# Batch 0's second x load on ScalarE's DMA queue, between the state and the conv taps

## Chip, cores and metric

The kernel runs on one core of one Trainium2 chip. The metric is the device time of one execution in microseconds. TensorE (PE) multiplies, VectorE (DVE) and ScalarE (ACT) do the elementwise work, GpSimd (POOL) a little of it, SyncE (SP) issues most transfers; ScalarE can issue transfers too, on a queue of its own.

## The reference

Attention between tokens and a small state in both directions, then a feed-forward layer with a convolution and a gate:

```python
def _attn_ref(x, state):                     # x (8,8,512,64), state (8,8,32,64)
    scores = scale * np.matmul(x, state.transpose(0, 1, 3, 2))
    a = softmax(scores)                      # with 1e-09 in the sum
    xread = np.matmul(a, state)
    scores2 = scale * np.matmul(state, x.transpose(0, 1, 3, 2))
    a2 = softmax(scores2)
    sread = np.matmul(a2, x)
    return np.concatenate([xread, sread], axis=2)

def _moe_ref(x, w_in, conv_w, w_out):        # x (8,576,512)... through H*D = 512
    h = np.maximum(x @ w_in, 0.0)            # (.., 1024)
    conv_out = sum(conv_w[k] * shifted(h, k) for k in range(3))   # along the tokens
    gate = 1.0 / (1.0 + np.exp(-conv_out))
    return h * gate @ w_out
```

The outputs of the attention, 544 tokens for each of 8 batches, are the x of the second function. The weights `w_in`, `conv_w` and `w_out` arrive as 8-byte floats and are turned into 4-byte ones on the chip.

## The kernel before

The work is cut into some 1,650 operations (a load, a group of matmuls, one elementwise instruction or a few). Each is registered with its engine in `Plan`, and a table of numbers, `ORDER`, sets the one order in which all of them are written out; every engine then carries out its own share in that order, each waiting for what it needs. A `v` behind a number puts an operation that ScalarE could do on VectorE. A negative number stands for that many matmuls on zeros (tile `idle`).

The part that matters here is the first microseconds. Operation 0 loads the state of batch 0 (`st`, 64 KB) on ScalarE's queue, 1 the rest of the state. Operations 98 to 103 are the conv taps: 98 loads `conv_w` (24 KB, tile `raw`) on ScalarE's queue, 99 and 100 are ScalarE's two steps of the conversion (L243 `w_abs`, L246 `w_round`), 101 to 103 VectorE's three (L249, L252, L260), which leave the taps in `cw`. Operations 120 and 121 load the two halves of batch 0's x (`xt`, 512 KB each, four heads in each). 123 and 124 are the scores of batch 0 for the first and the second half of the tokens (L316 `first_scores`); each needs the state and both x loads. 125v and 126v copy these scores to SBUF on VectorE (L196, two instructions each). After them come transposes (L484), a row maximum (L488), the shift by it (L494), the maximum `nm` for the other softmax (L335), and the exponentials on ScalarE (L340, L504). 14, 2, 16 and on are w_in loads on SP's queue and their conversions. A w_in load that takes over the `raw` buffer of the taps waits until they are done.

The reduction that makes `heads` (L182) is set up ahead of the plan and is placed by the scheduler among VectorE's operations.

Of the kernel before, what the change touches and what calls it, by code (L numbers as in the profile page):

```python
# [55 lines left out]
PSUM = dict(ps=8)  # L56

ORDER = """
120 0 98 99 100 121 101 102 -5 103 -7 123 125v 124 126v -1 14 15 17 -1 16 140 141 148 2 3 4 -1 149 20 21 5 142 150 32
# [101 lines left out]
def fused_kernel(ctx: ExitStack, tc: tile.TileContext, xT, xn, stT, w_in, conv_w, w_out, out):  # L161
    nc = tc.nc
# [10 lines left out]
    def buf(shape, dtype, tag, name, **kw):  # L173
        return (work if tag in UNEVEN else even).tile(shape, dtype, tag=tag, name=name, bufs=SBUF.get(tag) or SBUF[tag[:-1]], **kw)
# [114 lines left out]
    at, ps_s, nm2, e2, ps_t, e2t, s2, ps_r, rr, ps_f, xts, xxs = ({} for _ in range(12))  # L289

    def xt_load(i):
        b, g = divmod(i, NG)
        xts[i] = buf([P, 2, S], F32, "xt", f"xt_{i}")
        nc.sync.dma_start(xts[i], xT[b, :, 2 * g:2 * g + 2, :])

    def x_load(b):
        xxs[b] = buf([P, NCH, DM], F32, "xx", f"xx_{b}")
# [82 lines left out]
    def attention(b):  # L380
        for g in range(NG):
            i = NG * b + g
            add("SP", "load_xt", partial(xt_load, i), w=[("xt", i)])
# [566 lines left out]
```

## Time and profile before

| | us |
|---|---|
| time, median of 3 runs (lowest to highest) | 355.45 (355.43 to 355.82) |
| time of the profiled execution | 355.52 |
| its span, first to last instruction | 353.7 |
| TensorE busy | 347.9 (98%) |
| VectorE busy | 317.8 (90%) |
| ScalarE busy | 259.2 (73%) |

The times are of whole executions, the views of one profiled execution; what they show is read against that one's span. Times in the views count from the first instruction. A row of a timeline gives start, length, engine, line, operation, the tile written and the tiles read, and in brackets how long the engine was idle before it and what ended that. In the profile q1 is SP's queue of transfers and q10 is ScalarE's.

### The profile page before, as it was taken

How to read it: one execution, taken by the hardware profiler on the slowest of the kernel's cores; microseconds unless marked ns; L12 is line 12 of the kernel's file. 1: busy time of each engine (PE TensorE's matmuls, PEld its weight loads, DVE VectorE, ACT ScalarE, POOL GpSimd, SP SyncE). 2: the span in 40 equal slices, each digit the busy share in tenths (PEclk: the TensorE clock that was granted, in tenths of full speed). 3: DMA queues.
4: the chain of work that ended last, by engine and by line, in shares of the span. 5: the costliest groups of instructions: out<-in, count | busy, mean ns of one | idle time of the engine just before them, and what ended most of it. 6: DMA issues, size and time to landing. Idle time of an engine off the chain costs nothing.

```text
span 353.7 us, 6691 instructions
## 1 busy us (share of the span) xinstructions
PE 347.9 (98%) x2538; PEld 274.1 (77%) x2538; DVE 317.8 (90%) x542; ACT 259.2 (73%) x557; POOL 30.3 (9%) x90
## 2 busy tenths in 40 slices
PE   8999999999999999999999999999999999999995
PEld 7776668687788877878878887788788788688884
DVE  1999999999998999999999999999867897899881
ACT  2999999999884798599386578837637583576573
POOL 1000000010000000010040011402001020101110
PEclk9999999999999999999999999999999999999999
DMA  7998979204000242032120100001100200020004
GB/s 257 395 374 330 340 243 373 77 1 150 11 20 2 92 158 109 3 119 92 53 97 2 59 32 1 0 3 60 59 24 30 79 19 30 2 90 1 0 32 148
DMA packets 12816, 35.06 MB, mean 99 GB/s; under 512 B 1520, under 2 KB 3696, under 8 KB 11760
## 3 DMA queue, kind: packets, MB, share of 16 engines
q1 hardware_dynamic: 12208, 34.28, 26.9%
q8 instruction: 20, 0.33, 0.4%
q10 hardware_dynamic: 576, 0.35, 0.3%
q14 instruction: 12, 0.10, 0.1%
HBM read 25.71 MB, written 8.91 MB: 98 GB/s over the span
## 4 chain that ended last, share of the span: by engine, by line
PE 90%; DVE 3%; ACT 3%; issue 0%; DVEq 0%
PE acc L701 47%; PE ps_h L626 22%; PE ps_hs L611 4%; PE ps_u L544 4%; PE acc_t L701 3%; PE ps_r L362 2%; PE ps_h L633 2%; PE ps_t L349 2%; PE acc_c L701 2%; PE acc L709 1%; PE ps_s L306 1%; ACT raw L246 1%; DVE nm L335 1%; ACT hc L243 1%; DVE hc L252 1%; DVE wi L260 0%
## 5 line engine op out<-in xcount | busy, mean ns | idle before, releaser
L701 PE MATMUL acc<-wo,g 128*128 128x512 f32 x726 | 173.4, 391 | 0.0
L701 PEld LDWEIGHTS acc<-wo,g 128*128 128x128 f32 x726 | 135.6, 188 | 30.3 <-issue 1.3
L626 PE MATMUL ps_h<-a,u 128*128 128x512 f32 x336 | 82.2, 390 | 0.0
L626 PEld LDWEIGHTS ps_h<-a,u 128*128 128x128 f32 x336 | 62.8, 188 | 13.8 <-ACT o L715 0.8
L678 ACT ACTIVATE t<-t 128x512 f32<-128x512 f32 x64 | 40.2, 631 | 20.9 <-DVE t L674 20.7
L205 ACT ACTIVATE g<-t 128x512 fp32r<-128x512 f32 (+1 forms) x62 | 38.2, 619 | 20.3 <-DVE t L683 20.1
L674 DVE SCALAR_TENSOR_TENSOR t<-h,cw,t 128x512 f32<-128x512 f32 (+1 forms) x64 | 47.3, 745 | 1.8
L669 DVE SCALAR_TENSOR_TENSOR t<-h,cw,t 128x511 f32<-128x511 f32 x64 | 47.4, 745 | 1.4 <-ACT t L194 0.9
L208 DVE TENSOR_TENSOR g<-t,g 128x512 fp32r<-128x512 f32 (+1 forms) x62 | 41.4, 672 | 7.5 <-ACT g L205 7.1
L200 ACT ACTIVATE h<-ps_h 128x512 f32<-128x512 f32 x61 | 36.0, 597 | 12.6 <-PE ps_h L626 11.5
L683 DVE SCALAR_TENSOR_TENSOR t<-t,h 128x512 f32<-128x512 f32 (+1 forms) x64 | 42.3, 667 | 3.1 <-ACT t L678 2.8
L194 ACT ACTIVATE t<-h,cw 128x512 f32<-128x512 f32 x47 | 33.9, 723 | 0.7
L644 POOL COPY hs<-h 128x1 f32<-128x1 f32 x40 | 12.7, 326 | 198.8 <-ACT h L200 180.2
L715 ACT ACTIVATE o<-acc 128x512 f32<-128x512 f32 (+1 forms) x31 | 16.7, 548 | 10.4 <-PE acc L701 9.7
L644 POOL COPY h<-hs 128x1 f32<-128x1 f32 x40 | 17.0, 437 | 35.9 <-DVE t L683 13.5
L208 DVE TENSOR_TENSOR u<-ps_u,u 128x512 fp32r<-128x512 f32 x28 | 18.8, 680 | 0.4 <-ACT u L205 0.4
L205 ACT ACTIVATE u<-ps_u 128x512 fp32r<-128x512 f32 x28 | 15.8, 593 | 1.3 <-PE ps_u L544 1.2
L611 PEld LDWEIGHTS ps_hs<-sr,wi 128*128 128x128 f32 x128 | 14.7, 192 | 1.9 <-ACT t L678 0.8
L633 PE MATMUL ps_h<-p,u 128*128 128x256 f32 x64 | 14.8, 382 | 0.4 <-DVE u L208 0.4
L611 PE MATMUL ps_hs<-sr,wi 128*128 128x128 f32 x128 | 15.1, 277 | 0.0
L243 ACT ACTIVATE hc<-raw 128x512 f32<-128x512 f32 (+1 forms) x17 | 11.1, 666 | 5.3 <-DMA raw<-conv_w 4.0
L633 PEld LDWEIGHTS ps_h<-p,u 128*128 128x128 f32 x64 | 11.8, 190 | 3.3 <-ACT u L194 1.5
(100 smaller groups left out, 396.5 us busy)
## 6 DMA issues: line engine op xcount, KB each, us to landing
xt<-xT SPq DMA_DIRECT2D x16, 512.0 KB, 8.1
xx<-xn SPq DMA_DIRECT2D x8, 1024.0 KB, 6.0
out<-o SPq DMA_DIRECT2D x27, 256.0 KB, 2.1
raw<-w_in SPq DMA_DIRECT2D x8, 512.0 KB, 7.3
raw<-w_out SPq DMA_DIRECT2D x8, 512.0 KB, 8.3
out<-o SPq DMA_DIRECT2D x6, 128.0 KB, 1.7
out<-o_t SPq DMA_DIRECT2D x8, 64.0 KB, 1.7
st<-stT SPq DMA_DIRECT2D x1, 448.0 KB, 9.8
```

What stands on the lines that cost most here:

```text
L194: A.activation(dst, src, AF.Copy, scale=scale)
L200: A.activation(dst, src, AF.Relu, scale=0.5)
L205: A.activation(hi, src, AF.Copy)
L208: engine.tensor_tensor(lo, src, hi.bitcast(F32), op=ALU.subtract)
L611: PE.matmul(ps_hs[m, f][:, :NT], wi[:, k, f * P:(f + 1) * P], sr[m][:, k, :], start=(k == 0), stop=(k == NK - 1))
L626: PE.matmul(ps_h[i], u[j][:, g, fs], a[k][:, g, :], start=(n == 0), stop=(n == 3 * NG - 1))
L633: PE.matmul(ps_h[f][:, q * HS:(q + 1) * HS], us[0, f // 4][0][:, g, f % 4 * P:(f % 4 + 1) * P], half_of(pa[0], q)[:, g, :], start=(g == 0) ...
L669: V.scalar_tensor_tensor(t[:, 1:], h[:, :S - 1], cw[:, f, 0:1], t[:, 1:], op0=ALU.mult, op1=ALU.add)
L674: V.scalar_tensor_tensor(t[:, :n], h[:, 1:n + 1], cw[:, f, 2:3], t[:, :n], op0=ALU.mult, op1=ALU.add)
L678: A.activation(tt[i], tt[i], AF.Tanh, scale=0.25)
L683: V.scalar_tensor_tensor(tt[i][:, :n], tt[i][:, :n], 1.0, hd[i][:, :n], op0=ALU.add, op1=ALU.mult)
L701: PE.matmul(acc, g[j][:, cs], wo[:, k, f, :], start=(f == 0 and n == 0), stop=(f == NF - 1 and n == 2))
```

## The change

The second x load of batch 0 (operation 121, `xt_load(1)`) is issued by ScalarE and not by SP, and moves in the table from behind the taps' ScalarE steps to a place right behind the state load:

```diff
 ORDER = """
-120 0 98 99 100 121 101 102 -5 103 -7 123 125v 124 126v -1 14 15 17 -1 16 140 141 148 2 3 4 -1 149 20 21 5 142 150 32
+120 0 121 98 99 100 101 102 -5 103 -7 123 125v 124 126v -1 14 15 17 -1 16 140 141 148 2 3 4 -1 149 20 21 5 142 150 32
...
     def xt_load(i):
         b, g = divmod(i, NG)
         xts[i] = buf([P, 2, S], F32, "xt", f"xt_{i}")
-        nc.sync.dma_start(xts[i], xT[b, :, 2 * g:2 * g + 2, :])
+        (nc.scalar if i == 1 else nc.sync).dma_start(xts[i], xT[b, :, 2 * g:2 * g + 2, :])
```

On SP, at the start of the program, the two x loads stood ahead of the first w_in loads (`raw` from `w_in`; behind a tile's name its shape, partitions first):

```order
 L946 UNCONDITIONAL_BRANCH
 L294 DMA xt_91<-xT 128x1024
-L294 DMA xt_99<-xT 128x1024
 L239 DMA raw_143<-w_in 128x2x512
 L239 DMA raw_162<-w_in 128x4x256
```

The first w_in load now follows the first x load directly.

On ScalarE, at the same place, the second x load now stands between the load of the state and that of the conv taps (`raw` from `conv_w`, 128 rows of 48 words), whose conversion is the first work that ScalarE computes:

```order
 L946 UNCONDITIONAL_BRANCH
 L890 DMA st<-stT 128x128
-L239 DMA raw_94<-conv_w 128x48
+L294 DMA xt_94<-xT 128x1024
+L239 DMA raw_96<-conv_w 128x48
 L243 ACT_TABLE_LOAD
-L243 ACTIVATE hc_96<-raw_94 128x24
-L246 ACTIVATE raw_94<-raw_94 128x24
+L243 ACTIVATE hc_98<-raw_96 128x24
+L246 ACTIVATE raw_96<-raw_96 128x24
 L243 ACTIVATE hc_145<-raw_143 128x512
 L246 ACTIVATE raw_143<-raw_143 128x512
```

Only the x load is new in the row of work; the other signs are buffer numbers.

On VectorE, a little later, the four copies of the scores (`at` from `ps_s`), the first step of a w_in conversion (`hc`), `heads`, and the two row maxima (`m`):

```order
 L196 TENSOR_SCALAR at_117<-ps_s_0_0_118 128x256
 L196 TENSOR_SCALAR at_117<-ps_s_0_1_119 128x256
 L196 TENSOR_SCALAR at_117<-ps_s_1_0_130 128x256
+L182 TENSOR_REDUCE heads<-ident 128x4
 L196 TENSOR_SCALAR at_117<-ps_s_1_1_131 128x256
 L249 TENSOR_SCALAR hc_145<-hc_145 128x512
-L182 TENSOR_REDUCE heads<-ident 128x4
 L488 TENSOR_REDUCE m_0_155<-ps_x_150 128x16
 L488 TENSOR_REDUCE m_1_168<-ps_x_157 128x16
```

`heads` moved ahead of the fourth copy and of the w_in step.

## Rows read from the trace of the kernel before

**Rows 1.** The page's head.
```profile
span 353.7 us, 6691 instructions
```

**Rows 2.** Windows by stage: length, then each engine's busy time (instructions), clock, transfers.
```profile
core 0: us, PE busy (x) PEld busy (x) DVE busy (x) ACT busy (x) POOL busy (x), PEclk, DMA share, GB/s
8.00:20.00 12.00, 11.35 (x232) 8.53 (x232) 11.86 (x27) 11.24 (x25) 0.00 (x0) 1.00 1.05 396
20.00:32.00 12.00, 12.00 (x160) 8.49 (x153) 11.88 (x25) 12.00 (x28) 0.00 (x0) 1.00 0.91 338
40.00:60.00 20.00, 19.93 (x238) 14.36 (x231) 19.55 (x39) 19.39 (x46) 0.00 (x0) 1.00 0.85 306
60.00:200.00 140.00, 140.00 (x1007) 110.75 (x1006) 136.91 (x221) 109.35 (x249) 6.92 (x19) 1.00 0.20 71
```

**Rows 3.** The chain of waits, 0 to 40 us: start, length, what.
```profile
11.31 1.14 DVE nm L335
...
32.73 5.42 PE ps_h L633 x24
```

**Rows 4.** Timeline of VectorE, 6 to 18 us.
```profile
7.21 0.18 DVE L249 TENSOR_SCALAR hc<-hc 128x24 uint32<-128x24 uint32 x1 [6.23 <-ACT hc L243]
...
7.85 1.41 DVE L196 TENSOR_SCALAR at<-ps_s 128x256 f32<-128x256 f32 x4
...
9.51 0.28 DVE L182 TENSOR_REDUCE heads<-ident 128x4 f32<-128x128 f32 x1
...
11.23 1.21 DVE L335 TENSOR_REDUCE nm<-at 128x2 f32<-128x1024 f32 x1
```

**Rows 5.** Timeline of ScalarE, 6 to 18 us.
```profile
6.95 0.23 ACT L243 ACTIVATE hc<-raw 128x24 f32<-128x24 f32 x1 [4.02 <-DMA raw<-conv_w]
...
8.17 0.67 ACT L243 ACTIVATE hc<-raw 128x512 f32<-128x512 f32 x1 [0.87 <-DMA raw<-w_in]
...
12.48 0.72 ACT L340 ACTIVATE e<-at,nm 128x512 f32<-128x512 f32 x1 [0.16 <-DVE nm L335]
```

**Rows 6.** Timeline of TensorE, 6 to 18 us.
```profile
6.46 1.45 PE L316 MATMUL ps_s<-xt,st 64*32 64x256 f32 x32
...
8.41 1.34 PE L484 MATMUL ps_x<-ident,at 128*128 128x128 f32 x8
...
10.53 1.95 PE L494 MATMUL ps_s<-eight,m 128*32 128x128 f32 x64 [0.55 <-DVE m L488]
```

**Rows 7.** Timeline of all engines, 0 to 16 us: issues of transfers.
```profile
0.72 0.88 SPq L294 DMA_DIRECT2D xt<-xT  x2
...
1.16 0.46 ACTq L239 DMA_DIRECT2D raw<-conv_w  x1
...
1.64 6.71 SPq L239 DMA_DIRECT2D raw<-w_in  x6
```

**Rows 8.** Transfers issued from 0 to 1.14 us: count, KB, us to landing.
```profile
xt<-xT SPq DMA_DIRECT2D x1, 512.0 KB, 4.6
st<-stT ACTq DMA_DIRECT2D x1, 64.0 KB, 4.8
```

**Rows 9.** Transfers being issued from 1.17 to 1.5 us.
```profile
xt<-xT SPq DMA_DIRECT2D x1, 512.0 KB, 5.6
raw<-conv_w ACTq DMA_DIRECT2D x1, 24.0 KB, 5.8
```

**Rows 10.** The transfer being issued from 1.63 to 2.08 us.
```profile
raw<-w_in SPq DMA_DIRECT2D x1, 512.0 KB, 6.5
```

**Rows 11.** Queues from 2 to 4 us: packets, MB, share of the DMA engines.
```profile
q1 hardware_dynamic: 92, 0.38, 77.7%
q10 hardware_dynamic: 70, 0.04, 7.8%
```

**Rows 12.** All transfers from 4.75 to 6 us.
```profile
DMA packets 274, 0.50 MB, mean 401 GB/s; under 512 B 137, under 2 KB 142, under 8 KB 274
```

**Rows 13.** Waits from 0 to 60 us: total, times, longest.
```profile
ACT hc L243 <- DMA raw<-w_in: 1.1, 2, 0.9
```

## Prediction

> **What bounds the kernel now.** I read the page's head first: 353.7 us of span [rows 1]. Then the windows by stage, for where the span is fixed: from 40 to 60 us TensorE is busy 19.93 of 20 us and from 60 to 200 us all of 140 [rows 2]. From there on the kernel is a queue of matmuls; whatever delays the moment at which it fills delays the end by as much. Before that VectorE is busy 11.86 of 12 us from 8 to 20 and 11.88 of 12 from 20 to 32, ScalarE 11.24 and 12.00 [rows 2], and the chain of waits runs through them: it can be followed back to the row maximum `nm` on VectorE at 11.31 us, and enters TensorE for good at 32.73 us [rows 3].
>
> So the question is what sets the 11.31. On VectorE's timeline [rows 4] the engine idles 6.23 us until 7.21, waiting for ScalarE's first piece of the conv taps, and is busy from then on without a marked wait: the taps' three small operations, four score copies from 7.85, the reduction `heads` at 9.51, `nm` at 11.23. ScalarE's timeline [rows 5] shows why: its first operation starts at 6.95 after 4.02 us of waiting for the transfer of conv_w. The copies need no taps, they only stand behind them. The head of the chain is therefore the landing of the 24 KB of conv_w, not of x: the scores of batch 0 start at 6.46 and have ended at 7.91 (6.46 + 1.45) [rows 6].
>
> **When things land.** Issue times [rows 7] plus times to landing: first x load 0.72 + 4.6 = 5.3 us, first state load 4.8 us after its issue [rows 8]; second x load (issued at about 1.2) + 5.6 = 6.8, conv_w 1.16 + 5.8 = 6.96 [rows 9], which is the 6.95 of [rows 5]; first w_in load 1.64 + 6.5 = 8.14 [rows 10], which is ScalarE's next wait, 8.17 [rows 5]. The reader is to see that a load of 64 KB on ScalarE's queue takes as long as one of 512 KB on SP's queue beside it, and one of 24 KB as long as the next 512 KB. The packets say why: from 2 to 4 us SP's queue q1 moved 92 packets with 0.38 MB, ScalarE's queue q10 70 packets with 0.04 MB [rows 11]. The two queues take turns packet by packet, whatever a packet holds. Each of these loads has one packet for each contiguous row: x 128 of 4 KB, state 128 of 512 B, conv_w 128 of 192 B, the first w_in load 256 of 2 KB (from the shapes in the order rows).
>
> The Trainium skill, "DMA: Bandwidth & Descriptors", section "Queues, rings and completion order", says that a DMA engine goes round its queues but drains a whole packet of some 9 to 17 descriptors from one before it switches; by it, the state's 8 rows per DMA engine would follow x's 8 in one block. The trace disagrees: both queues' rows are moved in turn in those 2 us [rows 11]. What it would do here is the second rival.
>
> **The change part by part.** (1) *The order of arrival.* Now SP's queue holds the first x load and then w_in; ScalarE's holds the state, the second x load, conv_w. Up to 5.3 us nothing differs: 128 packets of x beside 128 of state. Then before, 128 packets of x (524 kB) ran beside 128 of conv_w (25 kB). Now the 128 of x run beside the first 128 of w_in (262 kB), and conv_w's 128 beside w_in's other 128. At 401 GB/s [rows 12] the 262 kB in between are 0.65 us: the second x load lands at 6.8 + 0.6 = 7.4. conv_w then ends beside the last packet of w_in, and since by then the same loads have been carried as before (x twice, state, conv_w, the first w_in), both land when w_in lands today, 8.14. That is 8.14 - 6.96 = **1.2 us later for conv_w**.
>
> (2) *What stands behind it.* ScalarE's first operation moves from 6.95 to 8.15, VectorE's from 7.21 to 8.4, the first copy from 7.85 to 9.05, `nm` from 11.23 to 12.4. The later x is hidden in this: scores end at 7.9 + 0.6 = 8.5, before the first copy; if conv_w were on time, it would show, since the first copies would then wait some 0.3 us for their half of the scores. ScalarE's work on the first w_in load moves from 8.17 to about 8.5 (two operations of 0.2 us go ahead of it); it has until `nm`, since its next bound operation, the exponential at 12.48, waits for that [rows 5]. From 8 to 32 us VectorE idles 0.26 us in all [rows 2], and those gaps end with work that shifts too; ScalarE's 0.76 lie ahead of 20 us, where it waits for loads and for VectorE, which sets the chain there. So I carry the whole 1.2 us through, with 0.9 as the bound if they all closed. In the first 60 us only two waits of a compute engine are for w_in, 1.1 us in all [rows 13], and none is for another load but conv_w; so no later transfer's wait is there to swallow the delay.
>
> (3) *Issue.* SP issues one load fewer (0.88 us for two [rows 7], so 0.44), and all of w_in is asked for 0.44 us earlier. Worth nothing: the first w_in load needs 6.5 us from issue to landing because it queues behind bytes. ScalarE issues one more, so conv_w is asked for at 1.6 in place of 1.16 and its table load goes 0.44 later; the 4.02 us of waiting cover both, and without that cover the price would be that 0.44. The sixth w_in load is issued once the taps are done (about 8.0 now, 1.64 + 6.71 less one issue); at 9.2 it still queues behind loads, so nothing is lost.
>
> (4) *`heads` ahead of the fourth copy on VectorE* [the order rows]. The same 0.28 us, a little earlier. The second group of transposes starts 0.28 us later, but what reads its result, the second row maximum, stands behind the first one on VectorE, as before. Cost nothing; if that cover went, 0.28.
>
> Sum: 355.52 us (the profiled execution, span 353.7 and 1.8 around it) + 1.2 = 356.7; the median of the runs, 355.45, lies 0.07 below it, so **356.65 us**.
>
> **Rivals.** *First, not slower: the loads keep their pace.* If the two queues shared by bytes, ScalarE's 600 KB would be through when twice that had been carried, 1200 KB against the 1112 KB that precede conv_w today: 88 KB, 0.23 us, and the copies would start some 0.25 us later: 355.7. It decides at 0.7 us: if conv_w lands before 7.65, no change is measured. Against it stand the 92 and 70 packets [rows 11], and 64 KB taking 4.8 us [rows 8]. The Trainium skill's same page, section "Issuing engines are not separate DMA queues", says that issuing from two engines only saves issue time; taken alone that gives no loss at all, and this trace has no load to show it on. Chance 0.14.
>
> *Second: the queues switch only after a run of rows.* With runs of 16 rows of a DMA engine, all that it has of the first w_in load, conv_w would come after that load, the second x load and half of the second w_in load: 262 kB more at 401 GB/s, 0.65 us on top, 1.85 us later, 357.3. Against it, again [rows 11]. Chance 0.08.
>
> *Third: TensorE loses its clock in the wider gaps.* It would now wait for the second x load between two groups of scores, and 0.6 us before the transposes (they move from 8.41 to 9.6, the work ahead of them by 0.6 only); one wait of that length, 0.55 before the matmuls at 10.53, is there today [rows 6], and the granted clock of that stretch is 1.00 [rows 2]. At half speed the transposes (1.34 us) and those matmuls (1.95 us) would cost up to 3.3 us more, about half of it on the chain: 358.3. Chance 0.04.
>
> **How the numbers follow.** Forecast 0.70 (355.45 + 0.9 to 1.5: 356.35 to 356.95), rivals 0.14, 0.08, 0.04, and 0.04 for a gain that I have no mechanism for. A measurement of this kernel tells 0.2%, 0.71 us. Forecast, second and third rival are slower by more, 0.82, of which I give 0.01 to a part of the forecast that closes up: slower 0.81, same 0.15, faster 0.04. The range takes the forecast, the second rival with a margin, and the upper edge of the first: 355.8 to 357.5.
>
> **What would show it.** Right: ScalarE's first operation starts near 8.15 and VectorE's near 8.4, still ended by conv_w; in the early stretch the second x load and conv_w land at about 7.4 and 8.1; `nm` near 12.4 and the chain's entry into TensorE near 33.9, and a span near 354.9. Step 1 is wrong if conv_w lands before 7.6 (first rival) or near 8.8 (second); step 2 if `nm` shifts by 1.2 but the span by less, which would mean slack between 12 and 40 us that the windows don't show. The first copies waiting for scores would say that x, not conv_w, is late.

## The result and the profile after

| | before | after | ratio (95% interval) |
|---|---|---|---|
| time, us | 355.46 | 358.50 (358.29 to 358.84) | 1.0081 (1.0066 to 1.0096) |

The change makes the kernel 3.0 us slower. 1.2 us had been predicted, 356.65 in all, and the range ended at 357.5. The direction was right, the size wrong. Measured again, the changed kernel gave 358.12 and 358.34 us on two chips, and in one single execution on a third 356.9. The part on the slow stretch comes back to this spread, which bears on the missing 1.8 us.

The page's head of the changed kernel (profiled execution, 358.84 us):

```profile
span 357.1 us, 6691 instructions
```

Its transfers by the time of their issue (count, KB, us from issue to landing), first those from 1.17 to 1.5 us, then those from 1.63 to 2.08:

```profile
xt<-xT ACTq DMA_DIRECT2D x1, 512.0 KB, 7.5
raw<-w_in SPq DMA_DIRECT2D x1, 512.0 KB, 7.8
...
raw<-w_in SPq DMA_DIRECT2D x1, 512.0 KB, 8.8
raw<-conv_w ACTq DMA_DIRECT2D x1, 24.0 KB, 7.6
```

The second x load is issued at 1.17 and lands at 8.7, conv_w at 1.65 and lands at 9.3. Before, they landed at 6.8 and 6.96 [rows 9]. ScalarE's timeline (issues, then the first operation) shows who waits:

```profile
1.17 0.45 ACTq L294 DMA_DIRECT2D xt<-xT  x1
1.65 0.48 ACTq L239 DMA_DIRECT2D raw<-conv_w  x1
...
9.30 0.22 ACT L243 ACTIVATE hc<-raw 128x24 f32<-128x24 f32 x1 [5.86 <-DMA raw<-conv_w]
```

VectorE's timeline answers to [rows 4]:

```profile
9.56 0.18 DVE L249 TENSOR_SCALAR hc<-hc 128x24 uint32<-128x24 uint32 x1 [8.58 <-ACT hc L243]
...
10.19 1.08 DVE L196 TENSOR_SCALAR at<-ps_s 128x256 f32<-128x256 f32 x3
11.19 0.27 DVE L182 TENSOR_REDUCE heads<-ident 128x4 f32<-128x128 f32 x1
...
12.36 1.29 DVE L488 TENSOR_REDUCE m<-ps_x 128x16 f32<-128x512 f32 x2 [0.23 <-PE ps_x L484]
...
13.90 1.21 DVE L335 TENSOR_REDUCE nm<-at 128x2 f32<-128x1024 f32 x1
```

The chain's two landmarks of [rows 3]:

```profile
13.98 1.14 DVE nm L335
...
35.53 5.42 PE ps_h L633 x24
```

The reader is to see one delay handed on: conv_w, and with it ScalarE's first operation, 2.35 us late (9.30 against 6.95), the first copy 2.34 (10.19 against 7.85), `nm` 2.67, the entry into TensorE 2.80 (35.53 against 32.73), the end 3.4 in the span of this execution, the slowest of four, and 3.0 in the median. What this execution loses behind its entry into TensorE is for the most part one wait, for a later x load:

```profile
66.47 1.09 PE L306 MATMUL ps_s<-xt,st 64*32 64x512 f32 x16 [0.54 <-DMA xt<-xT]
```

In the profiles of the two repeats below TensorE is busy for all of the 60 us from 60 to 120, so this wait is no fixed part of the loss.

Two things in the profile had not been forecast for this. First, the transfers from 4 to 5.25 us, all of them and then by queue, before:

```profile
DMA packets 224, 0.45 MB, mean 357 GB/s; under 512 B 66, under 2 KB 124, under 8 KB 224
...
q1 hardware_dynamic: 116, 0.41, 83.0%
q10 hardware_dynamic: 108, 0.04, 12.8%
```

and after:

```profile
DMA packets 115, 0.19 MB, mean 152 GB/s; under 512 B 18, under 2 KB 65, under 8 KB 115
...
q1 hardware_dynamic: 58, 0.17, 69.9%
q10 hardware_dynamic: 57, 0.02, 10.5%
```

Less than half the bytes, on both queues alike. By 6 us this is over: from 6 us on the changed kernel moves 389 GB/s, as the next view shows. Second, TensorE's timeline and the windows by stage (their columns as in [rows 2]):

```profile
6.06 0.64 PE L316 MATMUL ps_s<-xt,st 64*32 64x256 f32 x8 [0.22 <-DMA st<-stT]
8.76 1.93 PE L316 MATMUL ps_s<-xt,st 64*32 64x256 f32 x24 [2.06 <-DMA xt<-xT]
...
13.20 1.95 PE L494 MATMUL ps_s<-eight,m 128*32 128x128 f32 x64 [0.21 <-DVE m L488]
```

```profile
6.00:9.00 3.00, 0.88 (x16) 0.38 (x24) 0.00 (x0) 0.00 (x0) 0.00 (x0) 0.90 1.05 389
9.00:12.00 3.00, 3.00 (x31) 1.77 (x16) 2.27 (x9) 2.65 (x7) 0.00 (x0) 0.53 1.06 390
12.00:15.00 3.00, 2.79 (x73) 2.50 (x71) 2.77 (x5) 1.36 (x3) 0.00 (x0) 1.00 1.06 379
```

TensorE waits 2.06 us for the second x load, and in the stretch behind it its granted clock is 0.53, close to the lower of its two levels; that is the third rival.

### The profile page after: what moved, and what is told of

Read it like the earlier page. It is cut to its first block, busy times and chain, and to the rows that moved or that the text cites. A ratio compares the mean times of both kernels' runs of the same rounds, so it can differ in the third digit from the quotient of the medians.

```text
span 357.1 us, 6691 instructions
## 1 busy us (share of the span) xinstructions
PE 348.6 (98%) x2538; PEld 274.2 (77%) x2538; DVE 318.1 (89%) x542; ACT 259.2 (73%) x557; POOL 30.2 (8%) x90
## 4 chain that ended last, share of the span: by engine, by line
PE 87%; DVE 3%; ACT 3%; DMA 2%; issue 1%; DVEq 0%
PE acc L701 46%; PE ps_h L626 21%; PE ps_u L544 3%; PE acc_t L701 3%; PE ps_hs L611 2%; DMA xt<-xT 2%; PE ps_r L362 2%; PE ps_h L633 2%; PE ps_t L349 2%; PE acc_c L701 2%; PE acc L709 1%; PE ps_s L306 1%; ACT raw L246 1%; DVE nm L335 1%; ACT hc L243 1%
## 5 line engine op out<-in xcount | busy, mean ns | idle before, releaser
L200 ACT ACTIVATE h<-ps_h 128x512 f32<-128x512 f32 x61 | 37.2, 616 | 12.7 <-PE ps_h L626 11.0
L194 ACT ACTIVATE t<-h,cw 128x512 f32<-128x512 f32 x47 | 34.7, 739 | 0.7
```

Of the source, the lines that this page charges most:

```text
L194: A.activation(dst, src, AF.Copy, scale=scale)
L200: A.activation(dst, src, AF.Relu, scale=0.5)
```

## The experiments

The theory going in: the order on the queues costs what was predicted, and the remaining 1.8 us come from the slow transfers between 4 and 5.25 us, which have a cause of their own. Rivals: the table's new order costs something by itself; ScalarE's queue is slow for such a load; the lost clock is the price.

### The order in the table, and the order on the queues

**The changed table alone**, the second x load back on SP's queue:

```diff
-        (nc.scalar if i == 1 else nc.sync).dma_start(xts[i], xT[b, :, 2 * g:2 * g + 2, :])
+        nc.sync.dma_start(xts[i], xT[b, :, 2 * g:2 * g + 2, :])
```

> The changed table, but the second x load stays on SP's queue. Queue theory (all of the loss comes from the transfers' queues): the time of before, 355.45 within 0.3, conv_w landing near 6.9 us. Order theory (the reduction that makes heads, moved ahead of the fourth copy, or another shift of the order costs part of it): 355.7 or more, with a wait of VectorE before the second row maximum.

Measured: 355.77 us, ratio 0.9999 (0.9989 to 1.0009), 360 GB/s from 4 to 5.25 us. All of the loss comes with the load's move to the other queue; the table alone costs nothing. `heads` falls back behind the w_in step here, so its move did not come from the table, and this run does not test it.

**The conv taps ahead of the second x load** on ScalarE's queue, otherwise the changed kernel:

```diff
-120 0 121 98 99 100 101 102
+120 0 98 121 99 100 101 102
```

> The second x load on ScalarE's queue, but behind conv_w. Theory A, only conv_w's lateness counts: conv_w lands near 6.9 again, and the time falls to the bound of the later x that the prediction gave, 355.7 to 356.0. Theory B, the second x load is itself nearly as late as conv_w (8.71 against 9.28 us in the changed kernel): x lands near 8.7 to 9.0, the first copies start near 9.4 in place of 10.19, and the time is 357.3 to 358.0.

Measured: 358.66 us, ratio 1.0085 (1.007 to 1.01): nothing is won, though ScalarE now starts at 7.92. On VectorE's timeline the copies stand behind x instead:

```profile
10.41 1.42 DVE L196 TENSOR_SCALAR at<-ps_s 128x256 f32<-128x256 f32 x4 [1.52 <-PE ps_s L316]
```

The slow stretch is there too (169 GB/s). Both cases had expected an earlier time. The second x load, now asked for at 1.65 us and behind conv_w, lands about 1 us later than in the changed kernel (its scores start at 9.73 against 8.76). So the run trades one lateness for another: it shows that early taps win nothing when x pays for them, not what x would cost at its place in the changed kernel.

**One queue for all of it**: the kernel before, with SP's first w_in load put between the two x loads, and only the state and the taps on ScalarE's queue:

```diff
-120 0 98 99 100 121 101 102 -5 103 -7 123 125v 124 126v -1 14 15 17
+120 0 98 99 100 14 121 101 102 -5 103 -7 123 125v 124 126v -1 15 17
```

> The kernel before, all x and w_in loads on SP's queue, but in the order first x load, first w_in load, second x load; ScalarE's queue as before. Theory R, the stall comes when the w_in load of 2 KB rows follows the first x load directly, on whichever queue the second x load is: below 250 GB/s from 4 to 5.25 us. Theory S, it needs two long loads on two queues at once: over 350 GB/s there, the second x load lands near 8.15 us as third load and conv_w near 6.9.

Measured in one execution: 359.36 us. The transfers from 4 to 5.25 us:

```profile
DMA packets 115, 0.19 MB, mean 152 GB/s; under 512 B 17, under 2 KB 65, under 8 KB 115
```

These are the changed kernel's 115 packets and its rate, with no load of x on ScalarE's queue. The theory that this queue is slow falls. What the slow kernels have in common is that SP's first w_in load, with rows of 2 KB, is asked for right behind the first x load, at 1.17 or 1.18 us.

**The taps at the head of ScalarE's queue** in the kernel before:

```diff
-120 0 98 99 100 121 101 102
+120 98 0 99 100 121 101 102
```

> The kernel before, with conv_w in front of the state on ScalarE's queue: the reverse of what the change did to conv_w. If conv_w's landing is what the head of the chain waits for, it lands near 5.5 us, the taps are done before the scores, the first copy starts when its scores end, near 7.4 in place of 7.85, nm near 10.8, and the time is 0.2 to 0.4 us below before's. If the scores bound it as well (the state now lands near 6.9): no change, 0.1 either way.

Measured: 355.62 us, ratio 0.9996 (0.9985 to 1.0007). conv_w lands at 5.2 in place of 6.96, and VectorE's copies then wait for the scores:

```profile
7.58 1.42 DVE L196 TENSOR_SCALAR at<-ps_s 128x256 f32<-128x256 f32 x4 [1.36 <-PE ps_s L316]
```

The copies start 0.27 us earlier, no more: behind the taps, state and x bind next. `nm` is 0.19 us earlier than before (11.04), and the interval is too wide to tell whether the time follows.

### The first w_in load

**A little later**: the changed kernel, where GpSimd clears half of that load's buffer first, so that it is asked for at 1.53 us in place of 1.18:

```diff
     def w_load(j):
...
+        if j == 2:
+            G.memset(raws[j][:, 0].rearrange("p n t -> p (n t)").bitcast(F32), 0.0)
```

> The changed kernel, but GpSimd clears half of the first w_in load's buffer once, so that this load is issued at about 1.5 us in place of 1.18, clearly behind the second x load (1.17). Theory O, the order in which the two loads are asked for decides which is made ready first: no stall, the second x load starts near 4.1 us and lands at 6.6 to 7.4, conv_w at 7.4 to 8.1, and the time is 356.3 to 357.0, the predicted one. Theory T, the stall does not depend on this order (only a delay of 2 us took it away): below 250 GB/s from 4 to 5.25 us and 358.0 to 358.8.

Measured: 356.75 us over nine executions, ratio 1.0032 (1.0022 to 1.0042), and the transfers from 4 to 5.25 us:

```profile
DMA packets 174, 0.40 MB, mean 320 GB/s; under 512 B 30, under 2 KB 83, under 8 KB 174
...
q10 hardware_dynamic: 135, 0.30, 64.2%
q1 hardware_dynamic: 39, 0.10, 23.9%
```

ScalarE's first operation and the chain's entry into TensorE (the lines of this kernel are numbered two higher):

```profile
7.88 0.23 ACT L245 ACTIVATE hc<-raw 128x24 f32<-128x24 f32 x1 [4.47 <-DMA raw<-conv_w]
...
33.74 5.42 PE ps_h L635 x24
```

The delay is 1.0 us at TensorE, and 1.3 in the time. On the same chip, in the same series, the kernel of the clock experiment below, which issues its loads as the changed kernel does, had 157 GB/s and 357.65 us. So 0.35 us at one issue remove the slow stretch, and what is left is about the predicted price. It stays open whether the time counts or the order: here w_in is asked for after the second x load (1.16), in the slow kernels at the same moment or before it. The share of x's queue (135 packets to 39) shows that a later w_in load also lets x run ahead, so this run is no pure measure of the order.

**Much later** (the same with the whole buffer cleared twice, asked for at 3.18 us):

> The changed kernel, but GpSimd clears the buffer of SP's first w_in load twice, so that this load and those behind it on SP are issued some 2 us later. Supply theory: the second x load's rows are ready right behind the state's, it starts to move near 4.3 us in place of 5.25 and lands at 6.7 to 7.0 us, conv_w at 7.0 to 7.3. Theory that ScalarE's queue is late by itself (a second load on it starts at 5.25 us whatever SP does): the x load still starts near 5.25 and lands at 7.3 to 7.6, conv_w behind it. w_in lands later in both, so the time itself says little.

Measured in one execution: 356.53 us, 375 GB/s, ScalarE's start at 7.49, TensorE entered at 33.40.

**Shorter and longer rows**: the changed kernel with another w_in load first, one of 512 rows of 1 KB, and one of 128 rows of 4 KB.

```diff
-103 -7 123 125v 124 126v -1 14 15 17 -1 16
+103 -7 123 125v 124 126v -1 2 14 15 17 -1 16
...
+103 -7 123 125v 124 126v -1 32 14 15 17 -1 16
```

> The changed kernel, but SP's first w_in load is the one of 512 rows of 1 KB, not that of 256 rows of 2 KB. Turns theory (the queues take turns row by row at about 390 GB/s, and the stall between 4 and 5.5 us has nothing to do with rows): the second x load runs beside 128 KB in place of 256 KB and lands at 8.71 - 0.33 = 8.4 us, conv_w near 8.7. Supply theory (rows are made ready load by load in the order of issue, whichever queue they are for, so the second x load's rows come behind all rows of the w_in load issued beside it): 256 more rows stand ahead, the x load starts to move later than the 5.25 us of the changed kernel by some 1.2 us and lands near 9.6 us, conv_w later than that.

> The changed kernel, but SP's first w_in load is one of 128 rows of 4 KB. In the run with 512 rows of 1 KB there was no stall between 4 and 5.25 us (384 GB/s against 152). Theory P, the stall belongs to the load that is ready at once beside the second x load (few rows, made ready before x's): with 128 rows the stall stays or the x load starts as late, below 250 GB/s from 4 to 5.25 us and x landing at 8.3 us or later. Theory Q, it belongs to the one load of 2 KB rows (where it lies in memory): no stall here, over 350 GB/s, and x lands near 5.3 + 2.6 = 7.9 us or, running ahead of w_in, near 6.6.

Measured in one execution each: with 1 KB rows 357.34 us, with 4 KB rows 358.77. Neither has the slow stretch (384 and 323 GB/s), while beside each, on the same chip and in the same series, a kernel with the first loads of 2 KB rows had it (169 in the run with the taps ahead, 157 in that with matmuls on zeros). ScalarE waits for the taps until 7.46 with 1 KB rows and until 9.27 with 4 KB rows, and TensorE for x 2.03 us with the latter. The longer the row that stands across from a row of x, the later x and the taps: so far the turns by rows hold. But they are not strict: with 1 KB rows ScalarE's queue moved 157 packets from 4 to 5.25 us and SP's 42, and conv_w was earlier than either theory had it. With 4 KB rows neither theory comes out whole: the rate is between their bounds, and the scores that need the second x load start at 8.39, about as late as the first theory has it.

### TensorE's clock

**Five matmuls on zeros** in TensorE's wait for the second x load, otherwise the changed kernel:

```diff
         for j in range(NP):
+            if q == 0 and j == NP // 2:
+                for _ in range(5):
+                    fill()
```

> The changed kernel with five matmuls on zeros between batch 0's score matmuls of the first and those of the second x load, where TensorE waits 2.06 us. They compute nothing that is used. If the clock costs what the trace of the changed kernel shows (TensorE at 1.2 GHz from 8.4 to 11.8 us, VectorE's second row maximum waiting for it): the granted clock stays 1.00, nm moves from 3.71 to 3.4 us behind the first copy, and the time is 0.3 to 0.5 us below the changed kernel's 358.5, 358.0 to 358.2. If the clock costs nothing on the path: 358.3 to 358.8.

Measured: 357.65 us, ratio 1.0057 (1.0042 to 1.0072), mean granted clock 1.00, transfers still at 157 GB/s. From the first copy to `nm` it takes 3.38 us, as before (7.85 to 11.23), against 3.71 in the first profile after:

```profile
10.09 0.75 DVE L196 TENSOR_SCALAR at<-ps_s 128x256 f32<-128x256 f32 x2
...
13.47 1.21 DVE L338 TENSOR_REDUCE nm<-at 128x2 f32<-128x1024 f32 x1
```

I first read the whole step from 1.0081 to 1.0057 as the clock's price. The repeats below don't bear that out: without the extra matmuls they gave 1.0067 and 1.0071, inside this run's interval.

### Does the slow stretch belong to the kernel?

Three pairs were meant to find which addresses or rows make it. **The halves of x in the other order** (addresses of the first x load changed), in the changed kernel:

```diff
-120 0 121 98 99
+121 0 120 98 99
...
-        (nc.scalar if i == 1 else nc.sync)
+        (nc.scalar if i == 0 else nc.sync)
```

and, in the kernel before:

```diff
-120 0 98 99 100 121 101 102
+121 0 98 99 100 120 101 102
```

> The changed kernel with the two halves of batch 0's x swapped: SP loads the second four heads first, ScalarE the first four. In HBM a partition's row of the first half is bytes 0 to 4 K of each 8 KB, that of the second half 4 K to 8 K, and the w_in load behind it on SP reads 2 K to 4 K of every 8 KB. Address theory (the stall comes when these w_in rows are read while rows of x at the same places of the 8 KB are still in flight): no stall now, over 300 GB/s from 4 to 5.25 us, the second x load lands near 7.4, conv_w near 8.1, and the time is 356.3 to 357.2. Row theory (two runs of 2 KB in each partition, made ready right behind the first load, are slow wherever they lie): 150 to 170 GB/s as in the changed kernel, and 357.8 to 358.8.

> The kernel before, with the two halves of batch 0's x loaded in the other order on SP's queue. Address theory: nothing is read beside the first half that clashes with it in either order, the same landings within 0.2 us and 355.4 within 0.5. If the slow first 2 us (206 GB/s) come from the first half's place in memory, it lands nearer 4.5 than 5.3 us.

Measured: 357.95 us, ratio 1.0062 (1.0042 to 1.0082), with 281 GB/s; and 355.69 in one execution with 302. The first lies between the two cases in its rate, is as slow in time as the changed kernel, and settles nothing: it ran on the chip of the run with the taps ahead (169 GB/s), but in a later series without the changed kernel beside it. The second shows no cost.

**Other columns in the first w_in load**: the changed kernel with its 2 KB rows from columns 512 to 767, and the kernel of 4 KB rows with those from columns 0 to 511.

```diff
+    pieces[2] = (w_in[:, 0:2, 512:768], pieces[2][1])
...
+    pieces[5] = (w_in[:, 1:2, 0:512], pieces[5][1])
```

> The changed kernel with one number different: its first load of w_in takes columns 512 to 767 of each row instead of 256 to 511, so that one piece of the product is computed with other columns of w_in (size, row length and place in the queue stay). It tells apart why transfers fall to 152 GB/s between 4 and 5.25 us in the changed kernel. Theory A (which addresses are read at once: the first load of x reads the first 4 KB of rows 8 KB apart, and the w_in load reads from the same first half of rows 8 KB apart): with columns from the second half there is no fall, over 300 GB/s from 4 to 5.25 us, the second load of x lands near 7.4 us and the conv taps near 8.1, and the time is about 356.7. Theory B (rows of 2 KB in a load right behind the first load of x, wherever they lie): the fall stays, at most 170 GB/s, conv taps near 9.3 us, time 358.3 to 358.8.

> The kernel of the run with 4 KB rows in the first load of w_in, with those rows taken from columns 0 to 511 of w_in instead of 512 to 1023, so that one piece of the product is computed with other columns of w_in. Theory A (addresses): reading from the first half of rows 8 KB apart, as the first load of x does, brings the fall back: at most 200 GB/s from 4 to 5.25 us, where that run had 323. Theory B (row length): 4 KB rows have no fall wherever they lie, about 320 GB/s, and the time is that run's, about 358.8.

Measured in one execution each: 357.19 us with 306 GB/s, and 357.4 with 312. Each theory missed once.

**Columns 0 to 255, other columns with the halves swapped, and the changed kernel once more** beside them. The first load's columns in the first two, the second with the halves of x swapped as above:

```diff
+    pieces[2] = (w_in[:, 0:2, 0:256], pieces[2][1])
...
+    pieces[2] = (w_in[:, 0:2, 512:768], pieces[2][1])
```

> The changed kernel with its first load of w_in taken from columns 0 to 255 of each row (one piece of the product is computed with other columns of w_in; size and row length stay). With columns 512 to 767 transfers from 4 to 5.25 us ran at 306 GB/s, with the kernel's own 256 to 511 at 152. Theory A (rows of 2 KB from the half of the 8 KB rows that the x load also reads): the fall comes, at most 200 GB/s, and conv taps land near 9.3 us, time 358.3 to 358.8. Theory B (only the kernel's own addresses, or a matter of chance): about 300 GB/s, conv taps near 8.5, time near 357.

> The kernel with the halves of x swapped between the queues (SP loads bytes 4 to 8 K of the 8 KB rows first), and its first load of w_in from columns 512 to 767, bytes 4 to 6 K of 8 KB rows (one piece of the product is computed with other columns of w_in). Halves swapped alone gave 281 GB/s from 4 to 5.25 us, the other columns alone 306. Theory A (the same half in both loads makes the fall): at most 200 GB/s, conv taps near 9.3 us, time 358 or more. Theory B (not the halves): around 300 GB/s, time 357 to 358.

> The changed kernel as it is, once more, beside the two others: whether the fall to 152 GB/s between 4 and 5.25 us comes in each execution on this chip. If it belongs to the kernel: 140 to 200 GB/s, conv taps near 9.3 us, time 358.3 to 358.8. If it comes by chance, this run may show 300 GB/s and a time near 357.

Measured in one execution each: 356.56 us with 329 GB/s, 357.94 with 347, and for the changed kernel itself 356.9, with this from 4 to 5.25 us:

```profile
DMA packets 146, 0.39 MB, mean 311 GB/s; under 512 B 30, under 2 KB 46, under 8 KB 146
...
q10 hardware_dynamic: 85, 0.23, 47.1%
q1 hardware_dynamic: 61, 0.16, 46.2%
```

No edit, and no slow stretch. That takes the ground from under the two runs beside it, where no edit was needed to be rid of it, and from the pair before them, which ran on one more chip, where the changed kernel itself was not run. They tell nothing of the cause. Nor does a single time tell much: 357.94 belongs to an execution that enters TensorE at 34.01, earlier than the 34.22 of the one with 356.9, and then waits 1.2 us for a later load (`xx` from `xn`).

**The changed kernel in five rounds, twice**, each time on another chip:

> The changed kernel as it is, in five rounds beside the kernel before. The first measurement gave 358.5 us (ratio 1.0081) with the fall of the transfers to 152 GB/s; one more execution beside two other kernels gave 356.9 us without it (311 GB/s), close to the 356.65 predicted. Theory A (the fall is a matter of the chip, or of where the arrays lie in one load of the program): all executions of this run agree within some 0.3%, either near 358.5 (ratio 1.0066 to 1.0096) or near 356.9 (ratio 1.003 to 1.005). Theory B (it comes by chance in each execution): the executions spread from 356.7 to 358.8.

> The changed kernel as it is, five rounds once more. So far two measurements had the fall (358.5 and 358.12 us, every execution above 357.7) and one single execution did not (356.9). If the fall goes with the chip or the load of the program: all executions here lie on one side, either 357.7 to 359.0 (142 to 157 GB/s from 4 to 5.25 us, ratio 1.0050 to 1.0096) or 356.4 to 357.4 (about 311 GB/s, ratio 1.003 to 1.0045). If it comes by chance in each execution, both kinds are among them.

Measured: 358.12 us (357.74 to 358.95), ratio 1.0067 (1.005 to 1.0084); and 358.34 us (358.06 to 358.96), ratio 1.0071 (1.0058 to 1.0084). The first one's transfers from 4 to 5.25 us:

```profile
DMA packets 108, 0.18 MB, mean 142 GB/s; under 512 B 17, under 2 KB 63, under 8 KB 108
```

and its window from 9 to 12 us:

```profile
9.00:12.00 3.00, 2.62 (x35) 1.46 (x34) 2.12 (x9) 2.55 (x6) 0.00 (x0) 1.00 1.07 390
```

The second one's profile shows 144 GB/s. In the three series no execution of the changed kernel is below 357.7 us, in all 16. So, by their times, the slow stretch does not come and go between executions of a series, and one load of the program, on one chip, did not have it; that was one execution, so chance is not ruled out. In the profile of the first repeat the clock stays at 1.00, while TensorE is entered at 35.41 us, as late within 0.12 as in the first profile after. So it does in the second repeat, behind a longer wait of TensorE, and TensorE is entered at 35.51:

```profile
9.12 1.07 PE L316 MATMUL ps_s<-xt,st 64*32 64x256 f32 x24 [2.38 <-DMA xt<-xT]
...
9.00:12.00 3.00, 2.65 (x34) 1.56 (x34) 1.97 (x8) 2.40 (x6) 0.00 (x0) 1.00 1.07 390
```

The lost clock is not what makes the kernel slow.

## Why the size was wrong, step by step

**What bounds the kernel, and step 2: right.** The taps' landing is the head of the chain, and its delay passes through VectorE, ScalarE and into TensorE without loss (2.35, 2.34, 2.67, 2.80 us). No slack took any of it up. That the later x is hidden held as well: the first copy starts 0.9 us behind ScalarE's first operation as before (0.89 against 0.90), so it stands behind the taps and not behind the scores.

**Step 1, the order of arrival: half of it held.** The single execution without the slow stretch is the forecast almost row for row. ScalarE's timeline there:

```profile
8.27 0.22 ACT L243 ACTIVATE hc<-raw 128x24 f32<-128x24 f32 x1 [4.87 <-DMA raw<-conv_w]
```

VectorE's:

```profile
9.16 1.08 DVE L196 TENSOR_SCALAR at<-ps_s 128x256 f32<-128x256 f32 x3
...
12.54 1.21 DVE L335 TENSOR_REDUCE nm<-at 128x2 f32<-128x1024 f32 x1
```

and the chain:

```profile
34.22 5.42 PE ps_h L633 x24
```

Predicted were 8.15, 9.05, 12.4 and 33.9, and 356.65 for the time against 356.9. It is these rows that count, not the nearness of one time: the kernel before alone spreads from 355.29 to 356.72 us in the two series of five rounds. The turns by rows are also seen in the changed kernel's first profile once transfers run at full pace; from 5.5 to 7.5 us, all and by queue:

```profile
DMA packets 269, 0.78 MB, mean 392 GB/s; under 512 B 5, under 2 KB 5, under 8 KB 269
...
q10 hardware_dynamic: 124, 0.49, 59.3%
q1 hardware_dynamic: 145, 0.30, 40.6%
```

124 packets of x's queue beside 145 of SP's (5 of them under 512 B and rows of neither load): neither equal bytes (first rival) nor runs of 16 rows (second rival).

**The step that failed** is step 1's second sentence, "Up to 5.3 us nothing differs", and the 401 GB/s that the sum used from there on. It took the loads as the only thing that moves and the rate as given. In the timed series the rate from 4 to 5.25 us was 152, 142 and 144 GB/s, against 357 before: 0.19 MB in place of 0.45 in the first of them. The first x load itself lands at 0.72 + 5.1 = 5.8 us there, not at 5.3. What that cost can be read from the bytes carried by a given moment: by 6 us and until conv_w has landed, first in the execution without the slow stretch (8.27 us), then in the first profile after (9.30 us):

```profile
DMA packets 458, 1.15 MB, mean 192 GB/s; under 512 B 33, under 2 KB 161, under 8 KB 458
...
DMA packets 1192, 2.02 MB, mean 244 GB/s; under 512 B 208, under 2 KB 680, under 8 KB 1192
...
DMA packets 399, 0.87 MB, mean 145 GB/s; under 512 B 32, under 2 KB 160, under 8 KB 399
...
DMA packets 1316, 2.14 MB, mean 230 GB/s; under 512 B 211, under 2 KB 800, under 8 KB 1316
```

By 6 us 0.28 MB are missing, 0.72 us at the 390 GB/s of the stretch behind it. When conv_w lands, 0.12 MB more have been carried; x, state and taps are the same in both, so these are bytes of w_in that went ahead of the taps, 0.31 us. Together that is the 1.03 us between the two at ScalarE's first operation (8.27 to 9.30). At TensorE the two are 1.31 us apart (34.22 to 35.53), with the lost clock in it. So of the 2.80 us at TensorE about 1.5 are the order on the queues, predicted as 1.2, and 1.3 the slow stretch with all that follows it; this split is an estimate, since it sets single executions of different series against each other.

**Step 3 failed with it.** It put the earlier issue of w_in at nothing ("Worth nothing"), because w_in queues behind bytes. For w_in itself it won nothing (it lands at 1.18 + 7.8 = 9.0 us in place of 8.14). But the place that w_in got by it, right behind the first x load and level with the second, is the one at which the slow stretch was seen. With w_in asked for 0.35 us later the same load order ran at 320 GB/s in place of 157 and took 356.75 us in place of 357.65 on the same chip, where the slower of the two even had TensorE's clock kept up.

**Third rival: it came, and its price was wrong.** The clock did fall in the gap, in the profile of the first series (0.53 from 9 to 12 us). It cost about 0.33 us on the way to `nm` (3.71 less 3.38), not the 1.6 us that the rival gave, because only the rest of the scores and the transposes ran at the lower level, mostly beside VectorE's copies; in the profiles of the two repeats it stayed at 1.00 and the kernel was as slow. In the times it can't be seen: in the first repeat the executions with a mean granted clock of 0.995 took 358.08 to 358.95 us, those with 1.00 took 357.74 and 358.84. The rival's 358.3 lies near the measured time by accident.

**Step 4: right.** `heads` ahead of the fourth copy costs nothing: with it there, and the clock at 1.00, the first copy and `nm` are 3.38 us apart (9.16 to 12.54 in the execution without the slow stretch), as in the kernel before.

**What stays open** is why the transfers are slow there. Shown: in the runs that have it, the w_in load of 2 KB rows comes right behind the first x load, on whichever queue the second x load lies; 0.35 us of delay of that load was enough to be rid of it, and so was another load in its place, with rows of 1 KB or 4 KB (one execution each); and on one chip the changed kernel as it is had none (one execution). Whether chip, place of the arrays in memory, something in how the program was loaded, or chance decides, no run here tells.

The Trainium skill, "DMA: Bandwidth & Descriptors", section "Issuing engines are not separate DMA queues", has it that a second issuing engine saves issue time only. The runs agree in so far as the queue's name didn't matter (the one-queue run has the same slow stretch); they disagree with taking that for no change in time: what the move put behind and ahead of each load cost 0.7 to 0.8%.

## What to carry to other kernels

When a transfer is moved, write down what is then beside and behind each load, row by row, and what takes the freed place: here the gap on SP's queue was filled by a load nobody was waiting for, and it delayed those that were waited for. A small load at the end of a queue can be the head of the whole chain; ask where it lands, not how big it is. And a result that rests on a transfer rate in the first microseconds wants a repeat of the unchanged program beside the experiments from the start: without it the effect of an edit can't be told from a difference between chips or between loads of the program.

## What the runs showed that I had not expected

- All transfers together run at 181 to 227 GB/s from 2 to 4 us in the kernels here, and at 327 to 407 GB/s from 6 to 8; when the rise comes differs between kernels and, for one kernel, between series (357 and 152 GB/s from 4 to 5.25 us for the kernel before and after; 142, 144 and 311 for the latter in three more series).
- The queues' turns are not strict: from 4 to 5.25 us ScalarE's queue moved 135 packets while SP's moved 39, when w_in was asked for 0.35 us later.
- A wait of TensorE of 2.06 us was followed by a granted clock of 0.53 from 9 to 12 us; waits of 1.77 and 2.38 us at the same place in two other executions of the same kernel were followed by 1.00. The length of that wait alone does not decide it.
